# Another table of places for single instructions in a Branchformer block, forward and backward

## The chip, the cores and the metric

The kernel runs on one core of a Trainium2 chip. The metric is the device time of one execution in microseconds (us). The time before is the median of three runs.

A core has engines that run their own instruction streams: TensorE (PE: matrix products, with PEld for loading the stationary operand), VectorE (DVE), ScalarE (ACT), GpSimd (POOL), and SyncE (SP), which here issues most of the transfers. Each engine works its instructions off in the order in which they stand in its stream, and waits where an operand is not there yet.

## The reference

x is [2, 4000, 144], and there are eight outputs besides the first: the gradients of x and of the seven weights. The forward part, cut to what matters:

```python
xa = layernorm(x)
q, k, v = split(xa @ w_qkv)
p = softmax(q @ k.T * D ** -0.5)            # 4000 x 4000, for each of two batches
glob = (p @ v) @ w_att_out
u, g = split(gelu(xa @ w_mlp_in))
loc = (u * conv5(layernorm(g), dw_csgu)) @ w_mlp_out
m = concatenate([glob, loc])
out = x + (m + conv5(m, dw_merge)) @ w_merge
```

The kernel returns out and the products of grad_out with the derivative by each input.

## The kernel before, in words

**Tiles.** The 4000 tokens of a batch are 32 tiles of 125, so 64 tiles in all. After a head (weights folded, layer norm, transposes of x and grad_out), `phase_att` runs a loop over steps s, one tile to a step, with the stages of neighbouring tiles laid over each other. The scores are never kept: a step computes for one tile of queries the scores against all 4000 tokens, and at the same time the derivative of the scores of the tile before.

**One step**, with the lines that the prediction names:

- `jit_mm` (from L1575) makes the tile's queries and the row that the derivative is taken with; ScalarE copies them from PSUM into qb (L1581, L1590), and `jit_tr` (L1594) has SP issue a transposing transfer qt<-qb.
- `quad` makes the scores and the derivative products in PSUM, with matmuls of 128 rows (L1602) and of the remaining 16 (L1609). VectorE negates the scores into Pbuf and takes their minimum along the way (`S_min`, L1624, four to a step; nm L1626). ScalarE takes the exponential in place (`P_exp`, L1630, four to a step). SP issues the transposing transfer PT<-Pbuf in two halves (`P_tr`, L1634).
- `PdP`: ScalarE copies the derivative products into Sbuf (L1640) and VectorE multiplies them by Pbuf (L1642); SP transposes them, ST<-Sbuf (L1816).
- `Y_half` (L1651) multiplies PT with the normalized tokens, then come the small tail of the row (rl L1657, dj L1660, yn L1664, ty L1667, g L1671 and L1672) and on GpSimd QBs (L1673). `Z_half` (L1689) does the same with ST and ends in zn (L1693), which SP transposes (`zt_tr`, L1701).
- `X_group` (L1736) accumulates the part of the gradient that runs over the keys, from Sbuf and Pbuf with QBs; it is copied (ACT, L1740) or added (DVE, L1742) to acc.

The local branch (`local_units`, L524 on; for instance L577 to L671 on DVE) is cut into units and put between these. After the attention come `Merge` (transposes L1940 to L1946 out of Yr L2007, the products Hps of L2022, outputs po and o of L2120 to L2123, the gradient of the layer norm in dx_a L2132 and L2135 and dx_b L2142 to L2149) and `Final` (the gradients of the weights, from L2158 on, among them HT L2301 and L2302).

In the head, ScalarE writes normalized tokens xa_aug (L379; DVE and POOL share them, L381, L383), which TensorE transposes (L388), and scales weights into sWm (L233).

**What sets the order of the work.** The program is first written down in the order of the loops. Then `Planner.plan` (from L1228) gives each engine's stream its order. It makes groups of instructions (on PE up to eight score matmuls or up to sixteen others of one tile; elsewhere one instruction to a group), finds what each group must wait for, and lists them by modelled times, each group with a due time shifted by its kind (`LEAD`). Last, the table `MOVED` (L843 to L1073) is applied. For each engine it maps a place in the engine's order to the number of a group: the group goes to exactly that place, and the groups that the table does not name fill the other places in the order that the list gave. The order is then fixed by a chain of dependencies along each engine. `MOVED` thus changes no instruction and no operand, only which instruction comes behind which on one engine, and with it which semaphore an instruction waits for. SP's stream is part of it: its transfers are issued one after another, in the order of their places.

```python
m = self.MOVED[e]
put = set(m.values())
rest = iter([g for g in order[e] if g not in put])
order[e] = [m[q] if q in m else next(rest) for q in range(len(order[e]))]
```

Of the kernel before, what the change touches and what calls it, by code (L numbers as in the profile page):

```python
# [744 lines left out]
class Planner:  # L745
# [98 lines left out]
        "PE": {11: 163, 16: 167, 24: 19, 26: 20, 29: 21, 31: 22, 35: 25, 37: 26, 44: 27, 51: 334, 53: 28, 54: 342, 55: 29, 61: 31, 64: 33, 71: 37, 79: 38,  # L844
            82: 39, 85: 40, 86: 41, 91: 42, 93: 43, 95: 44, 99: 45, 105: 425, 113: 470, 114: 465, 121: 502, 141: 610, 143: 627, 145: 625, 157: 681,
            171: 786, 183: 819, 185: 853, 186: 820, 194: 902, 197: 915, 198: 923, 201: 930, 205: 958, 206: 959, 212: 972, 215: 973, 216: 1000, 228: 1054,
            229: 1075, 237: 1118, 247: 1169, 260: 1248, 261: 1253, 271: 1271, 284: 1373, 293: 1420, 295: 1416, 298: 1431, 302: 1470, 307: 1492, 308: 1473,
            310: 1511, 313: 1519, 321: 1550, 325: 1576, 327: 1589, 340: 1651, 342: 1652, 343: 1672, 345: 1694, 348: 1706, 351: 1723, 363: 1768, 383: 1910,
            387: 1911, 391: 1924, 407: 2011, 411: 2012, 419: 2088, 420: 2067, 423: 2098, 437: 2149, 439: 2170, 445: 2196, 452: 2210, 453: 2261, 457: 2249,
            459: 2303, 462: 2311, 464: 2320, 473: 2365, 489: 2463, 493: 2449, 494: 2467, 502: 2511, 513: 2561, 516: 2574, 521: 2605, 524: 2606, 525: 2654,  # L850
            532: 2713, 534: 2701, 537: 2702, 541: 2739, 552: 2787, 554: 2732, 556: 2845, 558: 2850, 560: 2851, 562: 2831, 570: 2929, 576: 2890, 577: 2957,
            584: 2983, 585: 3028, 588: 3021, 609: 3091, 610: 3095, 615: 3115, 616: 3156, 620: 3179, 621: 3173, 626: 3198, 628: 3190, 630: 3216, 634: 3247,
            637: 3242, 642: 3265, 645: 3283, 646: 3291, 651: 3299, 658: 3327, 662: 3339, 664: 3358, 678: 3400, 680: 3411, 687: 3427, 689: 3465, 693: 3489,
            700: 3519, 705: 3552, 710: 3520, 712: 3583, 717: 3587, 720: 3622, 733: 3629, 739: 3696, 740: 3726, 744: 3741, 747: 3766, 759: 3780, 762: 3818,
            764: 3826, 769: 3862, 776: 3898, 778: 3907, 782: 3930, 786: 3949, 790: 3988, 802: 4024, 804: 4044, 808: 4059, 824: 4127, 826: 4141, 829: 4184,
            840: 4216, 846: 4242, 850: 4278, 852: 4285, 854: 4290, 856: 4311, 858: 4317, 860: 4330, 869: 4368, 874: 4389, 883: 4425, 888: 4464, 894: 4498,
            896: 4503, 906: 4556, 913: 4595, 919: 4614, 921: 4654, 937: 4708, 941: 4748, 944: 4749, 952: 4780, 955: 4781, 971: 4893, 973: 4895, 975: 4915,
            984: 4987, 987: 4935, 991: 4974, 1000: 5027, 1008: 5078, 1010: 5067, 1013: 5081, 1022: 5130, 1032: 5174, 1034: 5195, 1037: 5230, 1046: 5274,
            1049: 5292, 1053: 5316, 1075: 5408, 1076: 5416, 1082: 5463, 1086: 5448, 1088: 5494, 1090: 5501, 1093: 5508, 1099: 5540, 1101: 5559, 1106: 5567,
            1109: 5589, 1118: 5642, 1129: 5671, 1132: 5701, 1137: 5726, 1156: 5811, 1160: 5881, 1167: 5886, 1169: 5926, 1172: 5896, 1177: 5919, 1181: 5984,  # L860
            1183: 5992, 1186: 6024, 1197: 6068, 1201: 6082, 1202: 6075, 1204: 6095, 1207: 6119, 1213: 6128, 1215: 6115, 1219: 6144, 1224: 6161, 1225: 6180,
            1230: 6211, 1233: 6206, 1234: 6207, 1236: 6230, 1238: 6242, 1242: 6266, 1247: 6270, 1251: 6271, 1255: 6292, 1264: 6319, 1267: 6331, 1272: 6317,
            1276: 6318, 1279: 6352, 1280: 6333, 1283: 6393, 1284: 6394, 1287: 6402, 1289: 6403, 1290: 6418, 1295: 6466, 1300: 6475, 1304: 6491, 1307: 6500,
            1308: 6478, 1309: 6493, 1316: 6518, 1318: 6519, 1319: 6527, 1321: 6528, 1323: 6543, 1324: 6544, 1328: 6596, 1334: 6621, 1338: 6622, 1339: 6958,
            1343: 6647, 1348: 6959, 1350: 6714, 1353: 6715, 1355: 6723, 1356: 6724, 1358: 6961, 1360: 6746, 1361: 6674, 1363: 6766, 1365: 6767, 1367: 6675,
            1372: 6789, 1376: 6900, 1377: 6903, 1380: 6852, 1381: 6853, 1383: 6875, 1384: 6905, 1387: 6906, 1389: 6930, 1391: 6931, 1393: 6934, 1399: 6941,
            1404: 6980, 1405: 6950, 1407: 6981, 1410: 6989, 1413: 6990, 1414: 6987, 1415: 7017, 1416: 6982, 1417: 7020, 1418: 7008, 1419: 6983, 1420: 7011,
            1421: 7024, 1422: 7056, 1425: 7027, 1427: 7031, 1430: 7071, 1433: 7108, 1434: 7110, 1435: 7148, 1437: 7111, 1438: 7115, 1441: 7149, 1445: 7084,
            1446: 7156, 1448: 7090, 1450: 7130, 1452: 7159, 1456: 7099, 1458: 7102, 1460: 7128, 1461: 7143, 1464: 7175},
        "DVE": {0: 68, 1: 9, 5: 94, 6: 95, 11: 91, 12: 106, 14: 111, 16: 99, 17: 104, 18: 110, 19: 101, 21: 102, 23: 107, 24: 105, 25: 148, 26: 98,  # L870
            29: 149, 31: 146, 33: 153, 35: 129, 36: 152, 37: 133, 38: 151, 40: 147, 41: 137, 42: 135, 43: 131, 45: 189, 46: 157, 48: 188, 50: 192, 52: 191,
            55: 186, 56: 185, 57: 172, 59: 190, 60: 176, 61: 195, 63: 164, 65: 178, 66: 211, 72: 219, 74: 203, 76: 229, 79: 237, 80: 235, 82: 266, 94: 335,
            95: 324, 109: 451, 110: 419, 115: 490, 117: 491, 118: 492, 121: 476, 122: 440, 123: 468, 124: 477, 126: 441, 127: 442, 128: 507, 134: 539,
            137: 472, 138: 556, 140: 563, 143: 528, 146: 529, 147: 530, 149: 575, 152: 550, 154: 560, 158: 601, 162: 641, 167: 636, 169: 651, 171: 652,
            176: 630, 177: 697, 179: 698, 181: 699, 182: 661, 183: 664, 184: 680, 185: 645, 188: 744, 189: 682, 190: 686, 191: 743, 193: 703, 198: 710,
            202: 688, 203: 709, 206: 711, 208: 712, 209: 722, 210: 718, 212: 733, 214: 748, 217: 749, 220: 764, 221: 755, 222: 752, 224: 793, 225: 826,
            226: 827, 234: 778, 235: 769, 237: 794, 238: 779, 243: 828, 246: 834, 247: 829, 249: 836, 253: 821, 256: 842, 257: 889, 258: 890, 259: 843,
            264: 831, 265: 852, 266: 844, 268: 848, 269: 861, 270: 845, 272: 846, 275: 880, 276: 874, 277: 871, 281: 882, 284: 916, 285: 886, 286: 908,
            288: 924, 289: 918, 291: 911, 296: 933, 298: 993, 299: 960, 301: 912, 302: 996, 304: 997, 305: 962, 306: 1028, 307: 1041, 309: 998, 314: 1042,
            316: 1043, 318: 1044, 319: 982, 320: 1045, 321: 1046, 323: 990, 326: 1047, 328: 1013, 329: 1048, 336: 1074, 338: 1049, 341: 1060, 342: 1063,  # L880
            345: 1035, 347: 1055, 349: 1076, 352: 1053, 353: 1065, 354: 1093, 355: 1135, 357: 1094, 359: 1087, 362: 1119, 363: 1095, 366: 1113, 368: 1137,
            370: 1138, 371: 1124, 373: 1139, 379: 1154, 380: 1170, 382: 1156, 384: 1189, 386: 1145, 391: 1172, 392: 1193, 393: 1144, 394: 1149, 395: 1146,
            397: 1147, 399: 1215, 400: 1213, 402: 1205, 403: 1217, 406: 1186, 408: 1208, 409: 1231, 412: 1223, 413: 1211, 415: 1236, 420: 1299, 422: 1298,
            425: 1247, 426: 1301, 431: 1343, 432: 1229, 433: 1278, 434: 1342, 436: 1344, 437: 1336, 438: 1345, 441: 1346, 444: 1347, 446: 1322, 449: 1306,
            451: 1323, 453: 1349, 455: 1350, 459: 1389, 463: 1355, 464: 1327, 465: 1363, 468: 1394, 469: 1374, 470: 1365, 472: 1339, 475: 1335, 476: 1377,
            478: 1400, 481: 1401, 483: 1385, 484: 1437, 486: 1438, 488: 1439, 493: 1429, 494: 1440, 496: 1452, 497: 1444, 498: 1497, 499: 1471, 500: 1496,
            505: 1445, 507: 1480, 508: 1446, 510: 1498, 511: 1455, 512: 1526, 514: 1499, 516: 1441, 521: 1482, 524: 1449, 526: 1510, 527: 1534, 530: 1533,
            531: 1536, 534: 1520, 537: 1489, 538: 1530, 542: 1601, 545: 1552, 548: 1508, 550: 1538, 553: 1577, 556: 1680, 558: 1681, 559: 1638, 560: 1605,
# [1693 lines left out]
```

## Time and profile before

| | before |
|---|---|
| median of 3 runs | 1217.23 us |
| lowest, highest | 1216.02, 1218.74 us |
| the profiled execution | 1215.52 us |
| its span | 1213.7 us |
| granted TensorE clock | 0.999 of full speed |
| busy, share of the span: PE, DVE, ACT, POOL | 96%, 89%, 77%, 21% |
| transfers: bytes, mean rate | 196.27 MB, 162 GB/s |

The profiled execution takes 1.8 us more than its span, which begins with the first and ends with the last recorded instruction. It is 1.7 us faster than the median. A row of the timeline reads: start in us, length in us, engine, line, operation, output<-inputs, shapes, how many were merged into the row, and in brackets the idle time of the engine just before it with what ended it. A row of the waits reads: engine and line that waited, engine and line waited for, then total us, times, longest.

### The profile page before, as it was taken

How to read it: one execution, taken by the hardware profiler on the slowest of the kernel's cores; microseconds unless marked ns; L12 is line 12 of the kernel's file. 1: busy time of each engine (PE TensorE's matmuls, PEld its weight loads, DVE VectorE, ACT ScalarE, POOL GpSimd, SP SyncE). 2: the span in 40 equal slices, each digit the busy share in tenths (PEclk: the TensorE clock that was granted, in tenths of full speed). 3: DMA queues.
4: the chain of work that ended last, by engine and by line, in shares of the span. 5: the costliest groups of instructions: out<-in, count | busy, mean ns of one | idle time of the engine just before them, and what ended most of it. 6: DMA issues, size and time to landing. Idle time of an engine off the chain costs nothing.

```text
span 1213.7 us, 36291 instructions
## 1 busy us (share of the span) xinstructions
PE 1168.9 (96%) x14352; PEld 947.3 (78%) x14352; DVE 1085.6 (89%) x3204; ACT 936.3 (77%) x1705; POOL 254.7 (21%) x413
## 2 busy tenths in 40 slices
PE   6999999999999998999999999999999999999998
PEld 4677777787877777887777777878777777899997
DVE  8579999999999998988799899999999997779625
ACT  6999788898897866777987888888888867646542
POOL 7110202211121123300111211113121222033530
PEclk9999999999999999999999999999999999999999
DMA  4668888898787889978878789888878789887752
GB/s 127 147 121 180 157 163 151 168 175 176 139 188 145 177 154 191 185 146 184 188 158 168 139 158 165 155 167 157 168 154 173 169 157 181 186 198 186 177 114 77
DMA packets 672637, 196.27 MB, mean 162 GB/s; under 512 B 647411, under 2 KB 666885, under 8 KB 672445
## 3 DMA queue, kind: packets, MB, share of 16 engines
q1 hardware_dynamic: 671336, 192.56, 78.5%
q8 instruction: 112, 1.84, 0.6%
q0 software_dynamic: 592, 1.18, 0.4%
q14 instruction: 59, 0.48, 0.1%
q10 hardware_dynamic: 538, 0.21, 0.1%
HBM read 23.14 MB, written 16.69 MB: 33 GB/s over the span
## 4 chain that ended last, share of the span: by engine, by line
PE 55%; DVE 20%; ACT 12%; DMA 8%; issue 3%; SPq 2%; POOL 1%; ACTq 0%; DVEq 0%; POOLq 0%
PE X L1736 15%; PE ps L1602 10%; PE yz L1651 7%; PE yz L1689 7%; DVE Pbuf L1624 5%; PE ps L1609 4%; DVE acc L1742 3%; DMA PT<-Pbuf 3%; ACT Sbuf L1640 3%; DVE Sbuf L1642 3%; ACT Pbuf L1630 3%; PE po L2120 2%; PE Hps L2022 2%; DVE l_prod L637 1%; DMA ST<-Sbuf 1%
## 5 line engine op out<-in xcount | busy, mean ns | idle before, releaser
L1624 DVE TENSOR_SCALAR_CACHE_REDUCE Pbuf<-ps 125x1000 bf16<-125x1000 f32 x256 | 306.4, 1197 | 29.1 <-PE ps L1609 28.2
L1640 ACT CAST Sbuf<-ps 125x1000 bf16<-125x1000 f32 x252 | 252.5, 1002 | 81.5 <-PE ps L1609 78.8
L1630 ACT ACTIVATE Pbuf<-Pbuf,nm 125x1000 bf16<-125x1000 bf16 x256 | 287.4, 1142 | 29.5 <-DVE nm L1626 28.8
L1736 PE MATMUL X<-QBs,Sbuf 125*125 125x144 bf16 x2048 | 298.4, 229 | 3.3 <-ACT acc L1740 1.7
L1736 PE MATMUL X<-QBs,Pbuf 125*125 125x144 bf16 x2048 | 293.3, 226 | 0.6 <-POOL QBs L1673 0.5
L1736 PEld LDWEIGHTS <-Sbuf 125*125 125x125 bf16 x2048 | 259.8, 137 | 27.5 <-issue 27.2
L1602 PE MATMUL ps<-xaT_m,qt 128*125 128x500 bf16 x1024 | 261.2, 375 | 10.6 <-DVE Pbuf L1624 7.2
L1736 PEld LDWEIGHTS <-Pbuf 125*125 125x125 bf16 x2048 | 260.8, 137 | 4.7 <-issue 4.2
L1742 DVE TENSOR_TENSOR acc<-X,acc 125x432 f32<-125x432 f32 (+1 forms) x373 | 201.1, 551 | 16.1 <-PE X L1736 15.7
L1642 DVE TENSOR_TENSOR Sbuf<-Sbuf,Pbuf 125x1024 bf16<-125x1024 bf16 x252 | 171.6, 687 | 2.5 <-ACT Sbuf L1640 2.0
L1602 PEld LDWEIGHTS <-qt 128*125 128x125 bf16 x1024 | 123.6, 137 | 54.0 <-issue 12.2
L1651 PE MATMUL yz<-xa_aug,PT 125*125 125x145 bf16 x2048 | 149.3, 228 | 5.3 <-DMA PT<-Pbuf 3.9
L1689 PE MATMUL yz<-xa_aug,ST 125*125 125x144 bf16 x2048 | 150.4, 228 | 3.6 <-ACT ty L1667 2.7
L1651 PEld LDWEIGHTS <-PT 125*125 125x125 bf16 x2048 | 137.4, 137 | 16.3 <-issue 9.2
L1689 PEld LDWEIGHTS <-ST 125*125 125x125 bf16 x2048 | 139.7, 138 | 11.6 <-issue 8.7
L1673 POOL TENSOR_TENSOR QBs<-g,g 125x144 bf16<-125x144 f32 x64 | 33.9, 529 | 415.2 <-ACT g L1672 312.2
L1609 PEld LDWEIGHTS <-qt 16*125 16x125 bf16 x1024 | 36.3, 128 | 98.8 <-issue 98.8
L1609 PE MATMUL ps<-XR,qt 16*125 16x500 bf16 x1016 | 110.9, 420 | 0.0
L637 DVE TENSOR_TENSOR l_prod<-ring,Wc 125x720 bf16<-125x720 bf16 x128 | 66.0, 529 | 0.0
L665 POOL TENSOR_SCALAR l_w<-ring,nc,c 125x144 f32<-125x144 bf16 x60 | 32.7, 550 | 135.5 <-DVE nc L661 60.0
L593 POOL TENSOR_TENSOR rsr<-ve,mhalf 125x2 f32<-125x2 f32 x32 | 25.9, 809 | 142.3 <-DVE ve L592 123.2
L2147 ACT ACTIVATE t<-t,dx_c,rstd_x 125x144 f32<-125x144 f32 x64 | 28.8, 500 | 32.5 <-DVE t L2146 32.4
(547 smaller groups left out, 2073.5 us busy)
## 6 DMA issues: line engine op xcount, KB each, us to landing
Zn_d<-zn SPq DMA_DIRECT2D x64, 35.2 KB
Yn_d<-yn SPq DMA_DIRECT2D x64, 35.2 KB
ug_d<-ugr SPq DMA_DIRECT2D x32, 70.3 KB
PT<-Pbuf SPq DMA_TRANSPOSE x126
ST<-Sbuf SPq DMA_TRANSPOSE x126
go_h<-in_grad_out_dram SPq DMA_DIRECT2D x8, 252.0 KB
Yg<-Yn_d SPq DMA_DIRECT2D x8, 252.0 KB
Yg<-ug_d SPq DMA_DIRECT2D x8, 252.0 KB
```

What stands on the lines that cost most here:

```text
L637: nc.vector.tensor_tensor(prod[:, bi].rearrange("p a b -> p (a b)"), ring[:, a, p + bi:p + bi + 5, :].rearrange("p a b -> p (a b)"), W.Wc[ ...
L1602: mm = nc.tensor.matmul(pp[r // 2][:, r % 2, 0:CH], QT[i][:, 2 * h, 0:PB], bs(i)[0].xaT_m[:, c * CH:(c + 1) * CH], start=True, stop=False)
L1609: nc.tensor.matmul(pp[r // 2][:, r % 2, 0:CH], QT[i][rs, 2 * h + 1, 0:PB], xr, start=False, stop=True)
L1624: nc.vector.tensor_scalar(pv(Pbuf, i % NPB, c2), src, -1.0, 3.0e38, op0=ALU.mult, op1=ALU.min, accum_out=NM[i][:, c2:c2 + 1])
L1630: nc.scalar.activation(v, v, ACT.Exp, bias=NM[i][:, 4:5], scale=-1.0)
L1640: nc.scalar.copy(pv(Sbuf, i % NDB, c2), src)
L1642: nc.vector.tensor_tensor(sc, sc, pchunk(i % NPB, c2), op=ALU.mult)
L1651: nc.tensor.matmul(Y, PT[0:PB, j, 0:PB], S.xa_aug[:, j, 0:D + 1], start=(j == 0), stop=(j == NB - 1))
L1673: nc.gpsimd.tensor_tensor(QBs[:, i % NPB, 1, :], g0[:], g1[:], op=ALU.add)
L1689: nc.tensor.matmul(Z, ST[0:PB, j, 0:PB], S.xa_aug[:, j, 0:D], start=(j == 0), stop=(j == NB - 1))
L1736: nc.tensor.matmul(X[:, jj, :], l, r, start=(n_ == 0), stop=(n_ == len(ops) - 1))
L1742: nc.vector.tensor_tensor(av, X[:, 0:nj, :], av, op=ALU.add)
```

## The change

Only the table `MOVED` of the class `Planner` is replaced by another. Entries (place: group) on each engine:

| | before | after | in both, the same place and group | groups named in both |
|---|---|---|---|---|
| PE | 330 | 391 | 96 | 214 |
| DVE | 1272 | 1333 | 109 | 857 |
| Activation | 629 | 679 | 98 | 384 |
| Pool | 164 | 165 | 28 | 110 |
| SP | 507 | 520 | 36 | 348 |

The table came from another search, in which the times at which transfers land were scattered. The instructions are the same, 14352 matmuls among them, and so is everything else in the file; lines below the table move down by 16. The diff, cut to the first and last line of one engine's list:

```diff
     MOVED = {
-        "PE": {11: 163, 16: 167, 24: 19, 26: 20, 29: 21, 31: 22, 35: 25, 37: 26, 44: 27, 51: 334, 53: 28, 54: 342, 55: 29, 61: 31, 64: 33, 71: 37, 79: 38,
...
-            926: 7095, 927: 7098},
+        "PE": {8: 163, 22: 19, 25: 20, 28: 21, 30: 22, 35: 25, 37: 26, 52: 28, 54: 334, 55: 29, 59: 342, 63: 312, 69: 321, 78: 38, 79: 353, 83: 39, 86: 40,
...
+            922: 7162, 928: 7141},
```

To place the two orders beside each other, each engine's new order was laid on the times at which the old trace has the engine busy: the instruction at place q of the new order then has the time at which the old order's work up to that place was done. On that axis 7321 of the 14352 matmuls stand elsewhere by more than 0.05 us. The mean distance is 0.6 us on PE, 1.4 on DVE, 1.2 on ACT and 3.6 on POOL, and PE's largest is between 1100 and 1200 us. These distances tell where instructions went, and no times of the new kernel.

More of the change, by code (lines that the diff above doesn't have):

```diff
@@ L843 @@
     MOVED = {
[26 rows of a table removed]
-        "DVE": {0: 68, 1: 9, 5: 94, 6: 95, 11: 91, 12: 106, 14: 111, 16: 99, 17: 104, 18: 110, 19: 101, 21: 102, 23: 107, 24: 105, 25: 148, 26: 98,
[101 rows of a table removed]
-        "Activation": {2: 58, 7: 57, 11: 126, 12: 59, 13: 247, 16: 141, 20: 128, 21: 250, 23: 248, 24: 56, 26: 253, 28: 249, 31: 60, 35: 216, 37: 212,
[49 rows of a table removed]
-        "Pool": {0: 86, 1: 70, 2: 47, 3: 49, 4: 51, 5: 71, 7: 84, 8: 50, 10: 82, 11: 52, 12: 87, 15: 103, 17: 136, 18: 132, 20: 142, 27: 236, 28: 260,
[50 rows of a table removed]
[31 rows of a table added]
+        "DVE": {0: 9, 5: 94, 6: 93, 7: 95, 11: 91, 12: 106, 14: 109, 16: 99, 18: 101, 20: 102, 21: 105, 22: 108, 23: 107, 24: 104, 25: 98, 28: 149,
[106 rows of a table added]
+        "Activation": {2: 58, 7: 121, 13: 134, 14: 59, 16: 244, 19: 60, 21: 177, 25: 253, 26: 56, 27: 247, 28: 171, 29: 249, 32: 245, 34: 250, 36: 216,
[53 rows of a table added]
+        "Pool": {0: 83, 1: 85, 4: 87, 5: 51, 6: 50, 7: 48, 10: 53, 11: 86, 12: 69, 14: 52, 17: 136, 18: 132, 20: 142, 21: 179, 22: 175, 26: 214, 27: 260,
[52 rows of a table added]
     }
```

464 rows, old and new, of the table MOVED are left out of this document.

## The prediction

> **What bounds the kernel now.** I read the page first, then the busy time by stretches of the span, then TensorE's own waits, and then the timeline at each place where TensorE stood still.
>
> ```profile
> span 1213.7 us, 36291 instructions
> PE 1168.9 (96%) x14352; PEld 947.3 (78%) x14352; DVE 1085.6 (89%) x3204; ACT 936.3 (77%) x1705; POOL 254.7 (21%) x413
> PE 55%; DVE 20%; ACT 12%; DMA 8%; issue 3%; SPq 2%; POOL 1%; ACTq 0%; DVEq 0%; POOLq 0%
> ```
>
> TensorE is recorded busy in 1168.9 of 1213.7 us, so 44.8 us of it are idle, and no order of the same matmuls can win more than that. The chain that ended last goes through PE for 55% and through DVE for 20%: two engines share the bound. The stretches tell where each has it (columns: stretch, its length, then busy us and instructions of PE, PEld, DVE, ACT, POOL, the granted clock, the DMA share, GB/s):
>
> ```profile
> 0.00:50.00 50.00, 38.93 (x337) 24.95 (x338) 34.85 (x111) 35.60 (x85) 26.03 (x57) 1.00 0.56 136
> ...
> 150.00:450.00 300.00, 294.39 (x3512) 233.56 (x3511) 299.05 (x880) 252.25 (x451) 56.48 (x85) 1.00 0.84 164
> 450.00:700.00 250.00, 238.78 (x2878) 190.93 (x2876) 221.31 (x611) 197.17 (x343) 43.79 (x74) 0.99 0.86 171
> 700.00:950.00 250.00, 248.75 (x3001) 198.54 (x3000) 247.55 (x721) 216.78 (x390) 44.31 (x65) 1.00 0.82 160
> 950.00:1050.00 100.00, 95.46 (x1137) 74.74 (x1134) 89.08 (x240) 66.91 (x108) 20.98 (x34) 1.00 0.87 175
> 1050.00:1213.70 163.70, 157.11 (x2383) 149.06 (x2381) 105.55 (x395) 76.22 (x152) 49.68 (x77) 1.00 0.63 153
> ```
>
> From 150 to 450 and from 700 to 950 us VectorE is busy for 546.60 of 550 us. There it is the bound: the same instructions in another order can win at most the 3.4 us that are left, and each new wait of VectorE lengthens the kernel. Between 450 and 700 us both engines have slack (PE 11.22 us idle, DVE 28.69), and from 950 to 1050 too (4.54 and 10.92): here single waits set the pace, and places in an order can matter. In the head TensorE idles 11.07 of 50 us. From 1050 us on TensorE is the bound, with 6.59 us idle. What TensorE waited for (total, times, longest):
>
> ```profile
> PE ps L1602 <- DVE Pbuf L1624: 7.2, 14, 0.9
> PE yz L1651 <- DMA PT<-Pbuf: 3.9, 5, 1.9
> PE pt L388 <- ACT xa_aug L379: 3.4, 1, 3.4
> PE X L1736 <- ACT acc L1740: 1.7, 2, 1.0
> PE ps L1602 <- DMA qt<-qb: 1.6, 1, 1.6
> PE pm L1945 <- POOL Yr L2007: 1.4, 1, 1.4
> ```
>
> The waits are many and small. Transfers, which the new table's search scatters, end only 3.9 + 1.6 us of these waits: a table that is robust against late landings has little to win in this execution.
>
> **The change part by part.** It adds and removes no instruction. It gives other places to instructions on all five engines: about half of the matmuls stand elsewhere, most by under one microsecond of the old time axis. Every cost is therefore a wait that goes or a wait that comes, and I went through the places where the old trace has a wait, and those where the new order puts a reader ahead of its writer. A place is costed at what stands in front of it in the rows.
>
> *Head.* The transposes at L388 wait for ScalarE's xa_aug:
>
> ```profile
> 11.21 0.72 ACT L233 ACTIVATE sWm<-raw,cols 128x144 bf16<-128x144 bf16 x2 [1.38 <-DMA go_q<-in_grad_out_dram]
> 11.84 0.49 ACT L379 ACTIVATE xa_aug<-x_tp,lnnm,rstd_x 125x144 bf16<-125x144 bf16 x1
> 12.38 1.09 PE L388 MATMUL pt<-ident,xa_aug 125*128 125x125 bf16 x8 [3.44 <-ACT xa_aug L379]
> ```
>
> The new ACT order puts L379 ahead of the two L233, which take 0.63 us from start to start, and ScalarE was idle for 1.38 us before them. So between 0 and 0.63 + 1.38 = 2.0 us; I take **-1.0**, half, since a load issue stays in front.
>
> *594 to 599 us.* Two waits for copies of acc:
>
> ```profile
> 592.32 1.26 ACT L1630 ACTIVATE Pbuf<-Pbuf,nm 125x1000 bf16<-125x1000 bf16 x1
> ...
> 593.92 0.63 ACT L1740 COPY acc<-X 125x432 f32<-125x432 f32 x1
> 594.60 0.22 PE L1736 MATMUL X<-QBs,Sbuf 125*125 125x144 bf16 x1 [0.76 <-ACT acc L1740]
> 599.10 0.28 PE L569 MATMUL ph<-Wi,xaT_m 128*125 128x288 bf16 x1 [0.91 <-ACT acc L1740]
> ```
>
> The first copy now stands four places earlier, ahead of the exponential of 1.26 us, the second one place earlier. The whole is 0.76 + 0.91 = 1.67; I take **-1.2**, bounds 0 and -1.67. The exponential goes back by seven places, and behind it the transfer PT: that is the second rival below.
>
> *616 us.* The transposed queries came late, because three transposes went through SP's queue one after the other:
>
> ```profile
> 609.20 1.20 SPq L1701 DMA_TRANSPOSE zt<-zn  x1
> 610.51 1.66 SPq L1634 DMA_TRANSPOSE PT<-Pbuf  x1
> 612.27 1.24 SPq L1594 DMA_TRANSPOSE qt<-qb  x1
> 616.35 0.85 PE L1602 MATMUL ps<-xaT_m,qt 128*125 128x500 bf16 x3 [1.64 <-DMA qt<-qb]
> ```
>
> The new order issues zt sooner, which takes half of a 1.20 us issue out of the way: **-0.6**, bounds 0 and -1.64.
>
> *999 and 1004 us.*
>
> ```profile
> 997.70 0.60 DVE L1742 TENSOR_TENSOR acc<-X,acc 125x432 f32<-125x432 f32 x1
> 998.22 0.68 DVE L1642 TENSOR_TENSOR Sbuf<-Sbuf,Pbuf 125x1024 bf16<-125x1024 bf16 x1
> ...
> 999.04 0.36 DVE L1693 SCALAR_TENSOR_TENSOR zn<-yz,rl,ty 125x144 bf16<-125x144 f32 x1
> ...
> 999.46 1.17 PE L1651 MATMUL yz<-xa_aug,PT 125*125 125x145 bf16 x16 [1.18 <-DVE zn L1693]
> 1004.49 1.01 PE L1602 MATMUL ps<-xaT_m,qt 128*125 128x500 bf16 x4 [0.73 <-DVE Pbuf L1624]
> ```
>
> zn moves four places forward, past 0.60 + 0.68 us and two smaller ones, more than its 1.18; the negation behind 1004.49 moves one or two. **-1.8**, bounds 0 and -1.91.
>
> *1147 us.*
>
> ```profile
> 1147.13 0.63 PE L1945 MATMUL pm<-ident,Yr 125*80 125x125 bf16 x8 [1.40 <-POOL Yr L2007]
> ```
>
> Matmuls of L2022 now fill this place, and pm comes 5 us later: **-1.4**, bounds 0 and -1.40.
>
> Together **-6.0**, at most -8.6.
>
> *New waits.* At 684 us the wait is for the second half of PT:
>
> ```profile
> 674.32 4.65 SPq L1634 DMA_TRANSPOSE PT<-Pbuf  x2
> 679.54 1.80 SPq L1594 DMA_TRANSPOSE qt<-qb  x1
> ...
> 684.05 1.17 PE L1651 MATMUL yz<-xa_aug,PT 125*125 125x145 bf16 x15 [1.86 <-DMA PT<-Pbuf]
> ```
>
> The new SP order issues qt and zt ahead of both halves of PT, and ScalarE's copies of qb ahead of the exponential. The first half goes back by up to the two issues (1.80 + 1.20); the second was held by its exponential, so most of that is hidden behind it: **+0.6**, bounds 0 and +3.0. The Trainium skill, page "DMA: Bandwidth & Descriptors", section "Queues, rings and completion order", says that each DMA engine consumes the descriptors of a queue in ring order; by that PT also stands behind qt's bytes, 131 KB, which at the 171 GB/s of this stretch is an estimated 0.8 us, and the term would be +1.4. No row here separates the two.
>
> Elsewhere readers come ahead of their writers:
>
> ```profile
> 1041.72 1.00 ACT L1640 CAST Sbuf<-ps 125x1000 bf16<-125x1000 f32 x1 [0.51 <-PE ps L1609]
> 1108.15 0.51 ACT L2147 ACTIVATE t<-t,dx_c,rstd_x 125x144 f32<-125x144 f32 x1 [0.17 <-DVE t L2146]
> 1179.86 1.27 ACT L2301 COPY HT<-fpt 16x640 bf16<-16x640 bf16 x2 [2.46 <-PE fpt L2300]
> ```
>
> At four places from 1016 to 1050 us X matmuls stand about one copy of 1.00 us too early behind ScalarE. Whether the copies, too, come earlier cannot be read from places; I take half, **+2.0**, bounds 0 and +4.0. Near 1107 us the copy xaT_m now stands behind two L2147, 0.51 us each: **+0.9**, bounds 0 and +1.0. Near 1180 us the copies of HT stand behind L2147: **+1.0**, bounds 0 and +1.8 (1.27 + 0.51). Places between 150 and 450 where TensorE would wait by a microsecond I cost at nothing: VectorE hides them, busy 299.05 of 300; without that cover each costs its microsecond. Together **+4.5**, at most +9.8.
>
> The sum is -6.0 + 4.5 = -1.5 us on the profiled execution of 1215.52 us, whose span of 1213.7 us has 1.8 us around it that stay. The end itself, the last L2123, the store on SP and the end of the span, stands in the same order. The profiled execution lies 1.7 us below the median of the three runs, 1217.23, so the forecast for a median is 1217.23 - 1.5 = **1215.7**. The bounds of the terms alone reach from -8.6 to +9.8.
>
> **The rivals.**
>
> *Relief kept, new waits covered: 1211.2 (-6.0).* The new places are laid out together, so an early reader may have an early writer. For it: the waits that go are in stretches where neither engine is full. Against it: what is won ahead of 700 us leads into a stretch in which VectorE has 2.45 us of idle time.
>
> *The table changes nothing that shows: 1217.2.* Each wait that goes is met by the next one behind it: the row of 7.2 us in 14 waits shows that TensorE's idle time is spread over many small waits, and taking one away brings the next reader to its own writer.
>
> *PT lands later, step after step: 1223.* This is the slower side. Between 450 and 700 and between 950 and 1050 us TensorE already waits for PT (3.9 us in 5 waits). If SP issues qt or zt (1.2 us each) ahead of PT, or ScalarE puts the exponential behind copies, in many steps and not only at 684 us, each such step pays about the 0.6 us priced above. There are 64 steps, about 16 us each (256 negations of L1624, four to a step, within some 1040 us), so 350 us hold 22; half of them give 11 x 0.6 = 6.6 us; with the reliefs and the other new waits at about nothing, 1217.23 + 6. It decides when PT's landing falls more than the present slack behind its first reader, at ten steps or so. Against it: issue to reader is about as far apart in both orders where I looked.
>
> *VectorE blocked by GpSimd.* The profile shows that the two hardly meet now:
>
> ```profile
> L1642 DVE TENSOR_TENSOR Sbuf<-Sbuf,Pbuf 125x1024 bf16<-125x1024 bf16 x252 | 171.6, 687 | 2.5 <-ACT Sbuf L1640 2.0
> L1673 POOL TENSOR_TENSOR QBs<-g,g 125x144 bf16<-125x144 f32 x64 | 33.9, 529 | 415.2 <-ACT g L1672 312.2
> ```
>
> The mean of L1642 is 687 ns where single ones took 0.68 us (998.22): 7 ns more. GpSimd's instructions move by 3.6 us on average in the new order, more than those of any other engine. If they met VectorE at random in the two stretches that it bounds, where GpSimd is busy 100.8 of 550 us, 18% of some 135 L1642 would wait half of 529 ns, 24 x 0.26 = 6.3 us: **1223.5**. The Trainium skill, page "SBUF — State Buffer", section "Who interferes with whom", says that VectorE and GpSimd share a port pair under an exclusive lock: the later one blocks fully. The 7 ns show only that the old order avoids such meetings, not that the rule fails. Against this rival: a table that avoided them once may do so again.
>
> **How the numbers follow.** About 0.2%, 2.4 us, is what a measurement of this kernel can tell from no change: faster is below 1214.8, slower above 1219.7. The forecast has 0.38 (own range 1212.5 to 1219; of it 0.14 faster, 0.23 within, 0.01 slower), relief kept 0.24 (faster), no effect 0.09 (within), late PT 0.20 and blocked VectorE 0.09 (slower). That makes faster 0.38, within 0.32, slower 0.30. The range reaches from 1217.23 - 8.6, 1208.6, to 1223.5; it leaves out the case in which every new wait is paid in full and the rivals above 1223.5.
>
> **What would show it.** In the new profile: the waits for xa_aug L379 (3.4), acc L1740 (1.7), qt (1.6), zn (1.2) and Yr (1.4) gone or smaller; PT<-Pbuf near 4.5 us, and above 10 if the third rival holds; VectorE busy 299 of 300 between 150 and 450 us as now; L1642's mean at 690 ns, and above 710 if GpSimd blocks it; rows of X behind ScalarE's copies between 1016 and 1050 us, some 2 us. I am wrong if VectorE has new waits in its full stretches, which I have not costed, or if a few places hold gains of several microseconds that no wait of TensorE names.

## The result, and the profile after

The new kernel takes 1232.22 us in the median of four runs (1231.69 to 1236.18); the kernel before takes 1216.62 (four runs, 1215.94 to 1218.74). The ratio is 1.0132, with a 95% interval of 1.0107 to 1.0157: 15.6 us slower. Measured again on another chip (e16 below), the ratio was 1.0119 (1.0081 to 1.0158). The forecast was 1215.7 with a range up to 1223.5. The profiled execution of the new kernel took 1236.18 us, 4.0 more than its median, so its waits add up to somewhat too much.

The page of the new kernel, same lines as before:

```profile
span 1234.4 us, 36313 instructions
PE 1177.7 (95%) x14352; PEld 951.3 (77%) x14352; DVE 1087.7 (88%) x3204; ACT 936.9 (76%) x1705; POOL 258.2 (21%) x413
```

The instructions are the same. In a span that is 20.7 us longer VectorE is busy 2.1 us longer and ScalarE 0.6, so that nearly all of the added time is standing for these two. TensorE stands 11.9 us longer (56.7 instead of 44.8) and is recorded busy 8.8 us longer; the granted clock below accounts for the larger part of that. By stretches of the span (columns as in the prediction):

```profile
0.00:50.00 50.00, 40.73 (x354) 26.41 (x355) 36.04 (x112) 37.66 (x87) 25.10 (x56) 1.00 0.53 128
150.00:450.00 300.00, 286.92 (x3405) 226.72 (x3405) 292.06 (x848) 246.78 (x439) 55.92 (x82) 1.00 0.83 158
450.00:700.00 250.00, 237.47 (x2850) 189.45 (x2849) 219.36 (x614) 194.13 (x339) 45.27 (x76) 0.99 0.86 169
700.00:950.00 250.00, 246.38 (x2960) 196.11 (x2958) 246.59 (x712) 213.69 (x383) 44.19 (x65) 1.00 0.85 162
950.00:1050.00 100.00, 94.55 (x1096) 72.88 (x1094) 90.43 (x252) 69.62 (x121) 23.96 (x37) 0.98 0.85 163
```

From 150 to 450 us, where VectorE was busy 299.05 of 300 us, it is now busy 292.06, and does 848 instructions where it did 880. That is the stretch that was to hide new waits. The waits of TensorE in the new kernel:

```profile
PE yz L1667 <- DMA PT<-Pbuf: 16.3, 16, 4.0
PE ps L1618 <- DVE Pbuf L1640: 5.3, 11, 0.8
PE yz L1705 <- DMA ST<-Sbuf: 5.2, 8, 1.2
...
PE ps L1618 <- DMA qt<-qb: 3.8, 3, 2.4
...
PE pt L388 <- ACT xa_aug L379: 1.4, 1, 1.4
```

PT went from 3.9 us in 5 waits to 16.3 in 16, ST from 0.9 to 5.2, qt from 1.6 to 3.8. VectorE's waits between 100 and 960 us show where these land, first before, then after:

```profile
DVE Pbuf L1624 <- PE ps L1609: 10.4, 18, 1.5
...
DVE rl L1657 <- PE yz L1651: 5.3, 7, 2.0
```

```profile
DVE rl L1673 <- PE yz L1667: 15.8, 14, 5.6
DVE Pbuf L1640 <- PE ps L1625: 11.2, 19, 1.1
```

rl is the first instruction of VectorE that reads the product with PT. Its waits tripled; the negation's (Pbuf) rose by 0.8 us. Between 100 and 400 us VectorE had 1.0 us of waits in all in the old trace, 0.3 of it at rl and none at the negation; in the new one it has 8.1. The row before, then the rows after:

```profile
DVE rl L1657 <- PE yz L1651: 0.3, 1, 0.3
```

```profile
DVE rl L1673 <- PE yz L1667: 4.3, 6, 1.3
DVE Pbuf L1640 <- PE ps L1625: 2.7, 4, 0.9
```

When is the time lost? The median of how much later the same matmuls start in the new trace than in the old one, by their old time:

```
old time, us   60   180   300   400   580   620   700   880  1000  1040  1100  1200
later, us    -1.1   1.7   7.5  10.3   8.6  13.4  12.3  13.8  17.3  22.3  23.2  20.4
```

The head is 1.1 us ahead, some 9 to 10 us go between 100 and 400 us, 4 at 600, 8 from 900 to 1040, and the tail wins 2 to 3 back. The step at 600 us, as the timeline of the new kernel shows it:

```profile
603.49 2.34 SPq L1650 DMA_TRANSPOSE PT<-Pbuf  x1
605.24 1.29 ACT L1646 ACTIVATE Pbuf<-Pbuf,nm 125x1000 bf16<-125x1000 bf16 x1
605.94 1.21 SPq L1610 DMA_TRANSPOSE qt<-qb  x1
607.24 3.78 SPq L1650 DMA_TRANSPOSE PT<-Pbuf  x1
...
614.11 1.11 PE L1667 MATMUL yz<-xa_aug,PT 125*125 125x145 bf16 x9 [4.03 <-DMA PT<-Pbuf]
```

This is the exponential of the prediction's second place, the one that "goes back by seven places". It ends at 606.5, qt is issued ahead of PT, PT's issue takes 3.78 us, and TensorE stands 4.03 us. Against the old trace its end is 13.0 us later, PT's issue 9.7, and TensorE would have been there 7.3 later. Of the twelve waits for PT above 0.3 us, eleven have PT issued later against its reader than before, eight of them by more than 1 us (up to 5.4).

Behind three of the long waits TensorE also works more slowly. After the 4.03 us at 614, the 2.96 at 1019 and the 2.44 at 1055 (qt) the granted TensorE clock is half for some 3.4 us, after the last for twice that. The clock is the third number from the end of these rows (0.57, 0.57, 0.53), first of the new trace, then of the old one, which has a single such place, after the 1.86 us at 684:

```profile
614.00:618.00 4.00, 3.89 (x33) 3.85 (x34) 0.00 (x0) 0.88 (x2) 0.00 (x0) 0.57 1.14 255
1020.00:1024.00 4.00, 4.00 (x31) 2.46 (x29) 1.62 (x6) 0.24 (x1) 0.00 (x0) 0.57 0.52 110
1055.00:1062.00 7.00, 7.00 (x49) 5.46 (x50) 2.25 (x5) 2.02 (x2) 0.00 (x0) 0.53 0.87 197
```

```profile
685.00:689.00 4.00, 4.00 (x37) 3.73 (x36) 3.21 (x14) 1.74 (x6) 0.59 (x2) 0.57 0.81 184
```

By these rows 6.7 us of full clock are missing in the new trace (0.43 and 0.43 of 4 us, 0.47 of 7) and 1.7 in the old one: an estimate of 5 us of the 8.8 that TensorE is busy longer. They fall into the steps at 600 us and from 1000 to 1040; between 100 and 400 us the new trace has none. Why these waits are followed by half clock and others of like length are not (1.74 us at 247 here, 3.15 in e12), no run shows.

### The profile page after: what moved, and what is told of

The parts are those of the page before. It is cut to its first block, busy times and chain, and to the rows that moved or that the text cites. A ratio compares the mean times of both kernels' runs of the same rounds, so it can differ in the third digit from the quotient of the medians.

```text
span 1234.4 us, 36313 instructions
## 1 busy us (share of the span) xinstructions
PE 1177.7 (95%) x14352; PEld 951.3 (77%) x14352; DVE 1087.7 (88%) x3204; ACT 936.9 (76%) x1705; POOL 258.2 (21%) x413
## 3 DMA queue, kind: packets, MB, share of 16 engines
q0 software_dynamic: 592, 1.18, 0.6%
## 4 chain that ended last, share of the span: by engine, by line
PE 39%; DVE 12%; DMA 7%; ACT 4%; issue 2%; SPq 1%; POOL 0%; ACTq 0%; DVEq 0%; POOLq 0%
PE X L1752 9%; PE ps L1618 6%; PE yz L1705 4%; PE yz L1667 4%; PE po L2136 3%; DVE Pbuf L1640 3%; PE Hps L2038 3%; DMA PT<-Pbuf 3%; PE ps L1625 3%; DMA ST<-Sbuf 2%; DVE acc L1758 2%; DVE Sbuf L1658 1%; DMA qt<-qb 1%; ACT Sbuf L1656 1%; ACT Pbuf L1646 1%
## 5 line engine op out<-in xcount | busy, mean ns | idle before, releaser
L1667 PE MATMUL yz<-xa_aug,PT 125*125 125x145 bf16 x2048 | 152.2, 231 | 16.9 <-DMA PT<-Pbuf 16.3
L1667 PEld LDWEIGHTS <-PT 125*125 125x125 bf16 x2048 | 140.2, 139 | 29.2 <-DMA PT<-Pbuf 20.8
L682 POOL TENSOR_TENSOR A_dwc<-l_fl,A_dwc 128x512 f32<-128x512 f32 (+2 forms) x48 | 38.4, 799 | 78.0 <-ACT l_fl L681 73.8
```

What stands on the lines that cost most here:

```text
L682: nc.gpsimd.tensor_tensor(acc, fl[r0:r1, 0:n], acc, op=ALU.add)
L1667: nc.tensor.matmul(Y, PT[0:PB, j, 0:PB], S.xa_aug[:, j, 0:D + 1], start=(j == 0), stop=(j == NB - 1))
```

## The experiments

Theory A: the new order lets the transposing transfers land too late for their readers. Rivals are named where a run tells them apart. The kernel before was measured again with each group of runs; its medians were 1218.22 (e1 to e4), 1216.45 (e5 to e8), 1219.45 (e9 to e12), 1222.21 (e13 to e16) and 1218.01 us (e17, e18), so the ratios are what is compared. Exchanging the table of one engine alone was not tried. Edits name lines as in the kernel before. The rows of e3, e4, e11, e13, e14 and e17 have the lines of their own files, where rl is L1740, the product with PT L1734, the scores L1685, the negation L1707.

### Where along the kernel: e1, e2

Both tables stand in the file, and a list says how many places of which order come first:

```diff
-            order[e] = [m[q] if q in m else next(rest) for q in range(len(order[e]))]
+            tab = (laid(self.MOVED[e], order[e]), laid(self.MOVED2[e], order[e]))
+            for which, n in self.CUT[e]:
+                new = [g for g in tab[which][:n] if g not in got]
...
+    CUT = {"PE": [(1, 507), (0, 1467)], "DVE": [(1, 928), (0, 2662)], ...   # e1; e2: [(0, 508), (1, 1467)], ...
```

> The new order up to the point that the new kernel's trace reaches at 410 us, the old order for everything else. In the two traces the same instructions run 9.7 us later there. Theory A (PT, ST and qt land later for their readers under the new order, each such wait is paid at once and nothing gives it back): about 1226 us, +8 to +10. Rival B (a loss at VectorE's full stretch is given back between 450 and 700 us, where both engines have slack; the total is set elsewhere): within 3 us of before.

Measured: 1225.37 us, ratio 1.0046 (1.0026 to 1.0065), 7 us above before in the medians. By the ratio that is 3.2 to 7.9 us: less than the 8 to 10 that theory A asked, and just outside rival B's 3. What is lost up to there is not given back, but it is smaller than the lag of one trace said.

> The old order up to the point that the old trace reaches at 400 us, the new order for everything else. Theory A, the losses add up: +15.6 less the 9.7 of the first part, so about 1223 us, +4 to +8. Rival B (the loss sits after 400 us): +12 or more.

Measured: 1223.42 us, ratio 1.0041 (1.0023 to 1.0059). That is within theory A's 4 to 8 us; its rival's 12 falls. The two parts sum to 1.0087 where the whole has 1.0119 to 1.0132; whether the rest is scatter or the parts work on each other the intervals do not tell. That the parts work on each other is suggested by the trace of e2 (1218.43 us, the fastest of its runs), which has no step at 600 us: it loses nothing up to 800 and 5 to 6 us from 900 to 1100.

### Is it the transfers at all: e3, e4

Every instruction keeps its place, but transposes become plain copies of the same bytes:

```diff
-        nc.sync.dma_start_transpose(out=PT[:, a:a + w, :], in_=Pbuf[:, i % NPB, a * 128:(a + w) * 128])
+        nc.sync.dma_start(PT[:, a:a + w, :], Pbuf[:, i % NPB, a * 128:(a + w) * 128].rearrange("p (a b) -> p a b", b=128))
```

and so for ST, qt, zt and dhT.

> The old order on every engine, written out in full, with the attention phase's transposing transfers (PT, ST, qt, zt, dhT) made plain copies of the same bytes, so that the transposition is left out and the numbers in the outputs are others; every instruction keeps its place. It is the base for the next run. Both theories: below before by at most the transfer waits of its trace, 3.9 + 1.6 + 0.9 + 0.9 = 7.3 us, so 1209 to 1217 us.

> The new order on every engine with the same plain copies, so that the transposition is left out as in the run before. Theory A (landings of transposes): the distance to the old order with plain copies shrinks from 15.6 us to 3 us or less. Rival C (the new places on the engines themselves make readers wait for TensorE, VectorE and ScalarE; the transfers only show it): the distance stays at 12 us or more.

Measured: old order 1206.04 us (ratio to before 0.9887, 0.9865 to 0.9908), new order 1204.20 us (0.9879, 0.9858 to 0.9899). With plain copies the new order is not slower; the medians have it 1.8 us faster, which the intervals do not tell from nothing. The whole loss hangs on these transfers being transposes, and rival C falls. Nor does either trace have a stretch of half clock in the attention phase: where the long waits are gone, the half clock is too. Whether it is the landing of the transposes or how long they hold SP's queue, this pair does not tell. The waits for PT with the new order and plain copies, and VectorE's at rl (100 to 960 us):

```profile
PE yz L1734 <- DMA PT<-Pbuf: 0.3, 1, 0.3
```

```profile
DVE rl L1740 <- PE yz L1734: 2.4, 5, 0.7
```

16.3 became 0.3, and 15.8 became 2.4. The base e3 missed its own range of 1209 to 1217: the old order won 12 us, though TensorE named only 7.3 us of waits for these transfers. Of VectorE's waits between 100 and 960 us the three largest (rl, Pbuf, acc) fell from 22.1 to 14.8 us, and the old order's stretch of half clock is gone; that these make up the rest is argued, not shown.

### Which transfers: e5 to e8

The same edit on qt, zt and dhT alone (e5, e6), and on PT and ST alone (e7, e8).

> The old order with only the small transposes (qt, zt, dhT) made plain copies, so that their transposition is left out and the outputs' numbers are others; PT and ST stay transposes. Base for the next run: between the base with all copies plain, 1206, and before.

> The new order with only qt, zt and dhT as plain copies (their transposition is left out). Theory A1 (small transposes put ahead of PT and ST in the queue make these late, as the third rival of the prediction has it): at most 4 us above the old order with small plain copies. Theory A2 (PT and ST stand in one another's way, or the readers of PT and ST come closer to their issue; the small ones hardly matter): 9 us or more above it.

> The old order with only PT and ST made plain copies (their transposition is left out); qt, zt and dhT stay transposes. Base for the next run: about 1206 to 1210 us by both theories, since PT and ST carry most of the bytes.

> The new order with only PT and ST as plain copies (their transposition is left out). Both A1 and A2: within 3 us of the old order with the same plain copies, since what is late in the waits is mostly PT and ST. If instead 8 us or more stay, the small ones (qt, dhT) are late by themselves, and neither theory holds.

Measured, small ones plain: old order 1206.53 (0.9922, 0.9893 to 0.9950), new order 1217.27 (1.0010, 0.9995 to 1.0025): 10.7 us apart. Large ones plain: 1207.23 (0.9930) and 1205.98 (0.9919, 0.9890 to 0.9948): no difference. So the loss needs PT and ST as transposes. With the small ones plain 10.7 of 15.6 us stay, in ratios 0.0088 of 0.0119 to 0.0132: their share is a third at most, and the intervals do not tell it from none. A1, the prediction's own version with qt and zt in the way, falls as the main cause. A2's figure holds, but not its remark that the small ones hardly matter: making them plain wins 0.8% in the old order and 1.1 to 1.2% in the new, and TensorE's waits for PT fall to 8.3 us in the new order and to 1.6 in the old. So they make PT later in both orders. What A2 left open is which of its two halves: transfers slower, or readers closer.

### Earlier issue: e9 to e11

Places on ScalarE and SP only, at the waits of the new trace; for the wait at 614 us:

```diff
 ScalarE
+L1630 Pbuf<-Pbuf,nm
 L578 l_th<-l_z
 L579 l_a<-l_sq
...
 L604 dugr<-pd
-L1630 Pbuf<-Pbuf,nm
```

> The new order, but on ScalarE the last exponential ahead of the transfer PT stands 1 to 8 places earlier at ten places where the new trace shows TensorE waiting for PT (14.8 us of waits in that trace). Theory D (the new order issues PT late for its reader, mostly because the exponential stands behind other work): the waits shrink, 4 to 8 us below the new kernel's 1232, so 1224 to 1228. Rival E (the landings are stretched by the transposes in flight, wherever the issue stands; a wait that goes comes back at the next reader): within 3 us of 1232.

> The new order, but on SP the late transfers PT, ST, qt and dhT stand 1 to 3 places earlier where they had been ready and queued, at those of the waits where that is so (87, 130, 200, 375, 380, 935, 992, 1007 us and a few more). Theory D: 2 to 4 us below 1232. Rival E: within 2 us of it.

> Both edits: exponentials earlier on ScalarE and the transfers earlier on SP at the places where the new trace waits. Theory D: the sum of the two, 7 to 11 us below 1232, so 1221 to 1225. Rival E: within 3 us of 1232.

Measured: e9 1231.49 us, ratio 1.0115 (1.0091 to 1.0140); e10 1231.88, 1.0108 (1.0085 to 1.0130); e11 1228.10, 1.0083 (1.0062 to 1.0104). Neither alone differs from the new kernel beyond the intervals, as rival E has it. Both together stand 0.4 to 0.5% below the new kernel's two ratios, 4 to 6 us, between rival E's 3 and theory D's 7; against the interval of 1.0119 that is not clear of noise. e11's waits of TensorE say why it is not more:

```profile
PE ps L1685 <- DMA qt<-qb: 7.8, 4, 3.7
...
PE yz L1734 <- DMA PT<-Pbuf: 6.2, 9, 2.1
```

PT fell from 16.3 to 6.2, and qt rose from 3.8 to 7.8: on SP, and on ScalarE where qb's copies were passed, another transfer became late instead.

### The gains of head and tail: e12

```diff
+    CUT = {"PE": [(1, 117), (0, 1243), (1, 1467)], "DVE": [(1, 114), (0, 2374), (1, 2662)], ...
```

> The new order up to the point that its trace reaches at 60 us and from the point that the old trace reaches at 1055 us, the old order between. The two traces have the new order 1.1 us ahead at 60 us, and it wins back 2.4 us after 1060. If both gains are of their places alone: 1217 - 3.5, 1213 to 1215 us. If the head's gain is lost in VectorE's full stretch behind it, and the tail's gain was only lag made up: within 1.5 us of before.

Measured: 1222.71 us, ratio 1.0030 (1.0013 to 1.0048). Neither expectation: it is slower than before. The lag in its trace (1218.81 us, near its fastest run) is -1.0 us at 120 us, between -0.6 and 2.3 from 180 to 600, within 0.3 of nothing from 700 to 1050, and +3 at the end. The head's 1 us is lost in the stretch that VectorE fills. The tail costs some 3 us rather than winning 2; as it begins with a wait of 3.15 us for ST at 1065 us, just behind the seam of the two orders, it is not shown whether the tail's places or the seam cost this. None of these versions is better than before.

### Readers later, or issue later: e13, e14

e13 puts TensorE's readers behind the next groups; e14 takes the old order and sets 126 exponentials two places back.

```diff
 TensorE (e13, at 1019 us)
-L1651 yz<-xa_aug,PT
 L697 pw<-ring
 L1602 ps<-xaT_m,qt
+L1651 yz<-xa_aug,PT
```

> The new order, but on TensorE the reader of a late PT, ST or qt stands behind the next one to three groups at 22 places where the new trace waits (25 us of waits for transfers there in all). No transfer's place is touched. Theory D (too little room between issue and reader): 8 to 12 us below the new kernel of the same chip. Rival E (the landing queue is the bound; whatever fills the wait is followed by the same wait later): within 3 us of it.

Measured: 1241.34 us, ratio 1.0158 (1.0124 to 1.0192), beside 1.0119 (1.0081 to 1.0158) for the new kernel on the same chip (e16). Nothing is won; the median is 2.4 us higher, which the intervals do not tell from nothing. Yet TensorE's waits for PT are nearly gone (15.9 us in e16), while VectorE's at rl are not (16.8 in e16):

```profile
PE yz L1734 <- DMA PT<-Pbuf: 3.3, 9, 0.9
```

```profile
DVE rl L1740 <- PE yz L1734: 21.4, 15, 3.2
```

The wait moved one engine on. Giving TensorE's reader more room, theory D's remedy, does not help by itself; rival E's figure holds.

> The old order, but on ScalarE the last exponential ahead of every PT transfer (126 of them) stands two places later, some 1.2 us. In the old trace 19 of 126 readers of PT have under 5 us from issue to reader, and 18 more under 5.5. Theory D: about 30 to 40 new waits of half a microsecond, 10 to 20 us above before. Rival F (room is not what sets it; VectorE's and TensorE's queues take it up): within 4 us of before.

Measured: 1328.36 us, ratio 1.0866 (1.0824 to 1.0909): 106 us, far beyond both theories, on average 0.84 us for each of the 126 exponentials that went back by some 1.2 (an estimate from the length of what they passed). In that trace TensorE waits 43.0 us for PT in 29 waits, where the old one has 3.9. But the run does not measure the slack of the transfer alone. VectorE also reads the exponentials itself, in the product with Sbuf (L1642 of the kernel before), and waits for them there 28.5 us in 22 waits, 0.2 in the old trace:

```profile
PE yz L1734 <- DMA PT<-Pbuf: 43.0, 29, 5.3
```

```profile
DVE Sbuf L1725 <- ACT Pbuf L1713: 28.5, 22, 2.7
```

And half clock follows at more than ten places, where by the same estimate 25 us of full clock are missing. What the run shows is that the old order has little slack behind these exponentials, on both ways together.

### The transposes by themselves: e15, and the new kernel again: e16

A small kernel issues transposes on SP and reads each with a matmul, which starts when it has landed.

> A kernel that computes nothing of the reference (its outputs are zeros): transposing transfers of 2048 (P, like PT), 512 (Q, like qt) and 256 columns (Z, like zt) in the patterns P, Q, QP, ZQP, PP, PQ, PPQ, PQP, PQZP and a small store ahead of P, four times each, each followed by matmuls that read them. Theory E: the issue of a P behind other transposes is stretched (1.6 us alone, 3 and more behind two), and landing from its own issue grows from about 4 us alone to 6 and more. Theory D: landing from issue is the same, within 0.5 us, in all patterns.

Its timeline, a 512-column transpose (Q) ahead of a 2048-column one (P):

```profile
61.94 1.20 SPq L55 DMA_TRANSPOSE d0Q<-src  x1
63.23 1.92 SPq L55 DMA_TRANSPOSE d1P<-src  x1
64.39 0.29 PE L58 MATMUL ps<-d0Q 128*128 128x128 bf16 x1 [2.81 <-DMA d0Q<-src]
...
67.53 0.29 PE L58 MATMUL ps<-d1P 128*128 128x128 bf16 x1 [2.85 <-DMA d1P<-src]
```

Q lands 2.45 us after its issue began, P 4.30. Two P, one after the other:

```profile
117.30 2.07 SPq L55 DMA_TRANSPOSE d0P<-src  x1
119.42 2.44 SPq L55 DMA_TRANSPOSE d1P<-src  x1
121.84 0.29 PE L58 MATMUL ps<-d0P 128*128 128x128 bf16 x1 [4.89 <-DMA d0P<-src]
124.09 0.29 PE L58 MATMUL ps<-d1P 128*128 128x128 bf16 x1 [1.96 <-DMA d1P<-src]
```

The second P holds SP for 2.44 us instead of 2.07 and lands 4.67 after its issue. From its own issue a P lands after 4.3 to 5.1 us in all patterns without other traffic, the longest behind another P, and a Q after 2.5 to 3.1. That is a little more spread than theory D's 0.5 us and far from E's growth to 6 us and more. In the kernel the landing that was waited for took 6.9 us at 614, and in both orders mostly 5.5 to 6.7; other transfers go beside it there. That other traffic can stretch it shows at the start of e15, where stores of 1.15 MB of zeros are under way:

```profile
9.99 0.34 SPq L70 DMA_DIRECT2D out_dram<-z  x1
...
11.93 9.73 SPq L55 DMA_TRANSPOSE d0P<-src  x1
...
23.93 0.29 PE L58 MATMUL ps<-d0P 128*128 128x128 bf16 x1 [12.35 <-DMA d0P<-src]
```

12.0 us from issue to landing, and SP held for 9.73 of them. The next P, behind another such store, took 11.0 us, and two Q 9.3 and 8.6.

> The new kernel itself, as the base of this chip: 1.0107 to 1.0157 of before, about 1232 us.

Measured: 1238.95 us, ratio 1.0119 (1.0081 to 1.0158); as expected in the ratio.

### VectorE's place for rl: e17, e18

```diff
 VectorE (at 1020 us; 15 places)
-L1657 rl<-yz
-L1660 dj<-yz,rl,qb
 L671 dhr<-l_dd,gpr
 L1742 acc<-X,acc
 L1624 Pbuf<-ps
+L1657 rl<-yz
+L1660 dj<-yz,rl,qb
```

> The new order with the readers of the late transfers later on TensorE as in e13, and on VectorE rl (with dj and nd behind it) later at the 15 places where the new trace has VectorE waiting for the product with PT at rl (16 us in all). Theory G (a late PT costs what VectorE and TensorE stand; both must have other work): 6 to 12 us below the new kernel. Rival H (rl is early for those that wait for it, QBs and X; what is moved back comes back as a wait there): at or above the new kernel.

> The new order with exponentials and transfers earlier at the late places as in e11, and rl later on VectorE as in e17. e11 alone had a ratio of 1.0083 to before. Theory G: 1.000 to 1.004. Rival H: 1.008 or more.

Measured: e17 1242.18 us, ratio 1.0189 (1.0164 to 1.0215); e18 1234.90, 1.0144 (1.0115 to 1.0172), against e11's 1.0083. Rival H: in e17 VectorE's wait at rl fell to 6.3 us, and ScalarE's waits for rl (100 to 960 us) rose from 8.5 for QBs and 5.0 for g to

```profile
ACT g L1754 <- DVE rl L1740: 15.2, 10, 3.1
ACT QBs L1752 <- DVE rl L1740: 14.2, 8, 3.0
```

The lateness goes on down the chain. Three tries at giving the readers other places (e13, e17, e18) did not hide it; taking it away where it begins, at the landing (e4, e8), did.

## Why the prediction was wrong, point by point

- **What bounds the kernel.** Right in the reading: VectorE fills 150 to 450 and 700 to 950 us, and each new wait of VectorE there lengthens the kernel. The failed step contradicts that reading: **"Places between 150 and 450 where TensorE would wait by a microsecond I cost at nothing: VectorE hides them".** VectorE hides a wait of TensorE only as long as it has no reader of what TensorE brings late. rl is such a reader, in a fixed place of VectorE's order, and the negation, which reads the scores, is another. Between 100 and 400 us TensorE's waits for PT went from none to 5.5 us in 8, VectorE's waits at rl from 0.3 to 4.3 and at the negation from none to 2.7. VectorE went from 299.05 to 292.06 busy us, and 9 to 10 us of lag arose there. e1 shows that the new order up to 410 us alone costs 5.6 us by the ratio (3.2 to 7.9). The prediction's sign of being wrong, new waits of VectorE in its full stretches, is what came.
- **The transfers.** "Transfers end only 3.9 + 1.6 us of these waits", and so little was to be won or lost there. The same view has 0.9 for ST and 0.9 for dhT, which this leaves out; and even so that is what could be won at most by TensorE's waits: e3 shows that 12 us hang on these transfers in the old order. The sum left out what could be lost. The third rival had the right mechanism (PT lands later, step after step) and was given 0.20; its sign of recognition, PT above 10 us of waits, came at 16.3. It was mis-sized: 6.6 us for 11 steps at 0.6, in two stretches where it was thought to matter, 15.6 measured, about half of it in a stretch that it left out (e1 and e2: 1.0046 and 1.0041). By its own 6.6 it should read 1223.8, not 1223, and the part on 594 us points to it as the second rival where it is the third. It also had no term for the clock: three more stretches' worth of half clock behind long waits, an estimated 5 us in the new trace. What was held against it, "issue to reader is about as far apart in both orders", is true of the median (6.4 us before, 6.2 after for PT, from each of 126 issues to the first of the sixteen matmuls that read it, its wait not counted) and misses the tail: readers under 5 us behind their issue rose from 19 to 25, under 4 us from 3 to 5. Its detail, qt and zt ahead of PT on SP, is a third of the loss at most (e5, e6); the late exponential at 606 us is another way to the same lateness, and how the rest divides was not measured.
- **The sum for the rest, -1.5 us.** With plain copies, where landings are out, the new order stands 1.8 us below the old (no difference by the intervals). The terms, each by its row: the head's wait 3.44 to 1.4, forecast -1.0, and 1.1 us ahead at 60 us, but lost again by 100 us (in e12 by 250); acc 1.67 to 0.4, forecast -1.2; Yr's 1.40 gone, forecast -1.4; zn's 1.18 gone; qt at 616 us, forecast -0.6, gone there and back at others with 2.4 and 0.8. The new waits: at 684 us 1.86 became 1.40 where +0.6 was expected; of the X matmuls behind ScalarE's copies only 0.44 us showed, at 1033, where +2.0 was expected, while PT (2.96, at 1019) and qt (2.44, at 1055) stood in the same place; the two in the tail did not show.
- **GpSimd in VectorE's way.** Wrong, as its low chance had it. The row of the new kernel:

```profile
L1658 DVE TENSOR_TENSOR Sbuf<-Sbuf,Pbuf 125x1024 bf16<-125x1024 bf16 x252 | 171.6, 686 | 11.1 <-ACT Sbuf L1656 9.9
```

  686 ns, 687 before: the new order does not bring the two together either, so nothing here speaks for or against the lock.
- **The rule on ring order.** e15 has P behind Q landing 4.30 us after its own issue, and behind a small store (0.33 us) 4.3 as well: the 131 KB ahead of it cost nothing beyond their own issue of 1.2 us. The Trainium skill, page "DMA: Bandwidth & Descriptors", section "Queues, rings and completion order", says that descriptors are consumed in ring order; the trace of e15 is in line with it, in that the later transfer was still waited for after the earlier one had landed, in PQ too (0.23 to 0.32 us). The estimated 0.8 us on top did not come, where no other traffic was about; behind a P, four times its size, a Q took 0.2 to 0.7 us longer than the 2.45 with nothing ahead.

What stays open: how much of a landing in the kernel is other traffic in flight; whether the landing of the transposes or their hold on SP's queue makes the readers late; how many of the 15.6 us are half clock behind a wait rather than the wait; and whether the difference between 1.0087 (e1 and e2 together) and 1.0132 is more than scatter.

## What to carry to other kernels

Where engines run in fixed orders, a wait that another engine "hides" is free only until the next reader of the late result on that other engine; look up that reader and its place before costing a wait at nothing. For a table of places, do not compare medians of the time between a transfer's issue and its reader, but count the readers in the short tail, and look at who else reads the producer before taking a run that sets every producer back (e14) for the slack of the transfer. Look at the granted clock behind each long wait of TensorE. To find out whether transfers are to blame, make them plain copies with every instruction in its place: two runs separated here what six edits of single places (e9 to e11, e13, e17, e18) could not.

## What the runs showed of the hardware that was not expected

A 128x2048 transpose from SBUF to SBUF lands 4.3 to 5.1 us after SP begins to issue it, one of 512 columns after 2.5 to 3.1, whatever transposes stand ahead of them; but two issued into stores of 1.15 MB took 12.0 and 11.0 us and held SP's queue for 9.73 and 8.99. And waits of TensorE of 4.03, 2.96, 2.44 and, in the old trace, 1.86 us were each followed by 3.4 us or more at half the granted clock, while a wait of 1.74 us, and one of 3.15 in e12, were not.
